# Batch 2's x tiles 0 and 1 turned by DMA instead of TensorE, with its four o tiles planned one to three slots earlier

## The chip, the core and the metric

The kernel runs on one core of one Trainium2 chip. The metric is device time of one execution in microseconds (us): four runs of the kernel before gave 292.17, 292.19, 292.23 and 292.23 us, median 292.21. The granted TensorE clock was 1.0 throughout the profiled execution. Five engines work side by side, each through its own instructions in program order: TensorE (PE, with weight loads shown as PEld), VectorE (DVE), ScalarE (ACT), GpSimd (POOL) and SyncE (SP); here SP does nothing but issue DMAs.

## What is computed

Two stages follow each other. The first is linear attention per batch and head with an RMS norm over each head's 64 features, the second a LayerNorm and a two-layer feed-forward network with ReLU and a residual. The norm's scale commutes with ReLU, so the kernel applies 1/std only at the end (`finish`).

```python
kv  = einsum('bhsd,bhse->bhde', k, v)              # B=8, H=8, S=576, D=64
out = einsum('bhsd,bhde->bhse', q, kv)
x   = out / sqrt(mean(out*out, -1) + 1e-6) * g_norm   # heads side by side: [B, S, 512]
xn  = (x - mean(x)) / sqrt(var(x) + 1e-6) * g_ln
y   = x + relu(xn @ w_ch1) @ w_ch2                 # 512 -> 2048 -> 512
```

## The kernel before

**Tiling.** Each batch has 576 rows: four main tiles of 128 rows and a remainder of 64. The remainders of two neighbouring batches make one more tile (`rem_tile`), and four of these make a ninth block, "rem". A block of four tiles is 512 rows: `x_blk` holds x in float32, `xT_blk` the centred x in bfloat16, turned so that features lie on partitions, and `st_blk` sums for the norm.

**The path of one tile** (class `Tile`). `o` is four PE matmuls into a PSUM bank (L260), from q turned (`qt`) and from the batch's k-v product (`kv_pack`). `sq` squares it on ACT (L266), `red` sums per head on DVE (L287). Then `y` in turn: `rms` on ACT (L297), `inv` (L304) and the multiplication (L292) on DVE; `x` (L311, with L315 for the mean), `xc` (L321), all DVE. `var` is a squared sum on ACT (L329). Last comes `turn`, with two forms:

```python
if on_pe:   # 4 transposes on PE (L337) into the one "misc" bank, copied out by ACT (L339)
else:       nc.sync.dma_start_transpose(dst, self.xc_t)   # one DMA from SP (L341)
```

The turned tile is what the block's first matmul (`mm1`, L402) reads. Its results are cleared through ReLU by ACT (L405) out of three PSUM banks (`ps1`) into `m1`; `mm2` (L418) multiplies those by the second weights into two banks (`ps2`), and `finish` (L423, DVE) makes `o_sb`, which two SP DMAs (L436, L437) store.

**Per batch besides.** `load_batch` on POOL has six DMAs for k, v and q, after a one-element copy (L98, `gate`) that waits until the q of the batch before has been turned. `kv_of` (L235) is 40 PE matmuls and two ACT copies. `turn_q_dma` copies q on DVE (`q_p`, L201) and turns it with one DMA from SP (L203), which gives `qt`.

**The order** is written out by hand. `mm1` and `mm2` are cut into slots: `tick()` stands before each group of 16 matmuls of 128 columns (or 8 of 256, or 4 of 512), and issues whatever the agenda has for that slot number, ahead of the group. `plan_tile(s, make, turn_at, on_pe)` puts `o`, `sq` and `red` into slot s, `y`, `x` and `xc` into s+2, `var` into s+6 and `turn` into slot `turn_at`. Since every engine works in program order, a slot number sets the place on all of them at once.

The slots around the change are: `mm1(1)` 32 to 47, `mm2(1)` 48 to 63 (four slots to an output tile, so `finish` comes ahead of slots 52, 56, 60 and 64), `mm1(2, 0, 2)`, which reads tiles 0 and 1 of batch 2, 64 to 71, and `mm1(2, 2, 2)`, which reads tiles 2 and 3, 72 to 79. In these slots also stand `kv_of(2)` and `turn_q_dma(2)` at 36 and 36.5, `rstd_of(1)` (L410, L411) at 46, `load_batch(3)` at 47, `kv_of(3)` at 55, `turn_q_dma(3)` at 56.7, the remainder tile `rem_tile(1)` at 62 (turned by DMA at 69), batch 3's own o tiles at 65, 70, 75 and 80, and `load_batch(4)` at 68.

Below, t0 to t3 are batch 2's tiles, qt(b) the turned q of batch b, and o_sb(1,n) the n-th output tile of batch 1.

Of the kernel before, what the change touches and what calls it, by code (L numbers as in the profile page):

```python
# [14 lines left out]
def kernel(  # L15
# [183 lines left out]
    def turn_q_dma(b):  # L199
        q_p = kv_in.tile([128, JJ, H, D], bf16, tag="qp", bufs=2)  # L200
        nc.vector.tensor_copy(q_p.rearrange("p j h d -> p h j d"), q_in[b % NB])  # L201
        q_t = qt_pool.tile([128, JJ, HP, 128], bf16, tag="qt", name="qt")
        nc.sync.dma_start_transpose(  # L203
            q_t.rearrange("p j hp t -> p (j hp) t"), q_p.rearrange("p j h d -> p (j h d)"))
        qts[b] = q_t
# [35 lines left out]
    def new_block(n, bufs):  # L241
        x_blk = xpool.tile([128, 4, Dm], f32, tag=f"x{n}", bufs=bufs, name="x_blk")
        st_blk = xpool.tile([128, 3, 4], f32, tag=f"st{n}", bufs=bufs, name="st_blk")
        xT_blk = xpool.tile([128, nK, 512], bf16, tag=f"xT{n}", bufs=bufs, name="xT_blk")
        return x_blk, st_blk, xT_blk
# [98 lines left out]
    def main_tile(b, j, pool=None, tag="ops"):  # L344
        q_t, kvp = qts[b], held[b]
        if b not in blks:
            blks[b] = new_block("main", 3)
        return Tile([(slice(0, 128), lambda hp: q_t[:, j, hp, :], kvp)], blks[b], j, pool, tag)

    def rem_tile(b):  # L350
        mms = []
        for half, bb in enumerate((b - 1, b)):
            qt, kp = qts.pop(bb), held.pop(bb)
            mms.append((slice(half * 64, (half + 1) * 64),
                        lambda hp, qt=qt: qt[:, J, hp, :64], kp))
        if "rem" not in blks:
            blks["rem"] = new_block("rem", 1)
        return Tile(mms, blks["rem"], b // 2)

    def plan_tile(s, make, turn_at, on_pe):  # L360
        box = []

        def first():
            t = make()
            box.append(t)
            t.o()
            t.sq()
            t.red()

        def second():  # L370
            t = box[0]
            t.y()
            t.x()
            t.xc()

        def third():
            box[0].var()

        def fourth():
            box[0].turn(on_pe)  # L380

        at(s, first)
        at(s + 2, second)
        at(s + 6, third)
        at(turn_at, fourth)
# [72 lines left out]
    def at(slot, fn):  # L458
        agenda.setdefault(int(slot), []).append((slot, fn))
# [145 lines left out]

    at(36, lambda: kv_of(2))
    at(36.5, lambda: turn_q_dma(2))
    for j, s, tn in ((0, 46, 53), (1, 51, 58), (2, 55, 63), (3, 59, 68)):
        plan_tile(s, lambda j=j: main_tile(2, j), tn, True)
    plan_tile(62, lambda: rem_tile(1), 69, False)  # L610
    at(78, lambda: rstd_of(2))

    for b in range(3, B):
        s = 32 * b
# [69 lines left out]
```

## Time and profile before

| what | before |
|---|---|
| median of 4 runs | 292.21 us |
| the profiled execution | 292.23 us |
| its span in the profile | 290.4 us |
| PE busy | 280.4 us |
| DVE busy | 150.8 us |
| ACT busy | 155.5 us |
| DMA moved | 35.84 MB |

Times in the profile count from the start of the span; the execution's 292.23 us hold 1.83 us more than the span. A row of the timeline has start, length, engine, line, operation, operands and number of instructions, and in brackets how long the engine sat idle before it and what ended the wait. A PE row's length has the drain of the matmul pipeline in it, so it overlaps the row that follows: what an instruction costs PE is the difference of starts, not the length. The same holds in part for DVE and ACT.

### The profile page before, as it was taken

The page shows a single profiled execution, that of the slowest core. Times are in us where ns is not written, and L with a number is a line of the kernel's source. Part 1 is how long each engine was busy: PE and PEld are TensorE (multiplying, and loading weights), DVE is VectorE, ACT ScalarE, POOL GpSimd, SP SyncE. Part 2 cuts the span into 40 slices and gives each one's busy share as a digit, 9 for nine tenths or more (in the row PEclk, how much of TensorE's full clock was granted, in tenths as well). Part 3 has the DMA queues.
Part 4 walks back from the last instruction along what each step waited for, and adds up shares of the span by engine and source line. Part 5 has one row for each costly group of instructions (what it writes and reads, how often), then busy time and mean ns, then how long its engine had stood idle before and what let it go on. Part 6 is the DMA issues. An engine that isn't in the chain of part 4 may idle for free.

```text
span 290.4 us, 5777 instructions
## 1 busy us (share of the span) xinstructions
PE 280.4 (97%) x2294; PEld 159.4 (55%) x2320; DVE 150.8 (52%) x335; ACT 155.5 (54%) x341; POOL 41.0 (14%) x68
## 2 busy tenths in 40 slices
PE   7789999999999999999999999999999999999995
PEld 3579755995578754444444544444444444444444
DVE  5775028836996893666366935752578300220022
ACT  3467755885569931892189408920894066016500
POOL 8522520032050003200410023000000000000000
PEclk9999999999999999999999999999999999999999
DMA  7999999469789618994997279949202510131033
GB/s 216 203 206 201 201 202 219 105 105 194 141 146 204 100 42 150 211 171 89 150 201 108 49 145 200 165 77 168 54 18 54 110 36 0 38 81 27 2 72 72
DMA packets 63291, 35.84 MB, mean 123 GB/s; under 512 B 30749, under 2 KB 58269, under 8 KB 63265
## 3 DMA queue, kind: packets, MB, share of 16 engines
q0 software_dynamic: 28016, 17.76, 43.8%
q1 hardware_dynamic: 34736, 16.99, 29.4%
q10 hardware_dynamic: 512, 0.72, 0.7%
q8 instruction: 18, 0.29, 0.4%
q14 instruction: 9, 0.07, 0.1%
HBM read 36.71 MB, written 9.44 MB: 159 GB/s over the span
## 4 chain that ended last, share of the span: by engine, by line
PE 84%; DVE 6%; DMA 3%; ACT 2%; issue 2%; POOL 0%; SPq 0%; DVEq 0%; POOLq 0%
PE p L402 40%; PE p L418 38%; DMA v_in<-in_v_dram 2%; PE o_ps L260 2%; PE kv_ps L235 2%; DVE o_sb L423 1%; DVE ss L287 1%; DVE x_blk L311 1%; DVE y L292 1%; DMA out_dram<-o_sb 1%; ACT m L405 1%; PE tp L183 1%; DVE xc L321 1%; PE p L196 1%; ACT sq L266 0%
## 5 line engine op out<-in xcount | busy, mean ns | idle before, releaser
L402 PE MATMUL p<-xT_blk,w_sb 128*128 128x128 bf16 (+2 forms) x1017 | 131.7, 285 | 0.9 <-ACT m L405 0.3
L418 PE MATMUL p<-w_sb,m 128*128 128x512 bf16 (+2 forms) x590 | 126.9, 368 | 1.6 <-issue 0.8
L405 ACT ACTIVATE m<-p 128x512 bf16<-128x512 f32 x144 | 85.3, 597 | 41.8 <-PE p L402 39.7
L402 PEld LDWEIGHTS <-w_sb 128*128 128x128 bf16 x1024 | 78.5, 98 | 44.6 <-issue 1.1
L418 PEld LDWEIGHTS <-m 128*128 128x128 bf16 x608 | 56.8, 98 | 61.2
L423 DVE SCALAR_TENSOR_TENSOR o_sb<-p,rstd,x_blk 128x512 f32<-128x512 f32 (+2 forms) x38 | 27.4, 720 | 54.0 <-PE p L418 51.2
L266 ACT ACTIVATE sq<-o_ps 128x512 f32<-128x512 f32 x34 | 20.2, 595 | 41.2 <-PE o_ps L260 41.2
L329 ACT ACTIVATE dev<-x_blk,st_blk 128x512 f32<-128x512 f32 x36 | 25.7, 715 | 4.5 <-DVE st_blk L315 4.4
L287 DVE TENSOR_REDUCE ss<-sq 128x8 f32<-128x512 f32 x34 | 23.1, 678 | 8.4 <-ACT sq L266 8.4
L321 DVE SCALAR_TENSOR_TENSOR xc<-x_blk,st_blk,g_ln_sb 128x512 bf16<-128x512 f32 x34 | 25.6, 752 | 1.2
L292 DVE TENSOR_TENSOR y<-o_ps,inv 128x512 f32<-128x512 f32 x34 | 23.5, 692 | 2.8
L311 DVE SCALAR_TENSOR_TENSOR x_blk<-y,g_norm_sb 128x512 f32<-128x512 f32 x34 | 23.5, 692 | 1.2
L411 DVE RECIPROCAL rstd<-rstd 128x4 f32<-128x4 f32 x9 | 1.6, 174 | 39.3 <-ACT rstd L410 39.3
L304 DVE RECIPROCAL inv<-rms 128x8 f32<-128x8 f32 x36 | 7.2, 200 | 23.1 <-ACT rms L297 23.1
L98 POOL COPY gate<-qt 1x1 bf16<-1x1 bf16 x5 | 0.9, 178 | 114.8 <-DMA qt<-q_p 114.8
L297 ACT ACTIVATE rms<-ss,eps_sb 128x8 f32<-128x8 f32 x36 | 10.7, 297 | 9.8 <-DVE ss L287 9.1
L260 PEld LDWEIGHTS <-qt 128*128 128x128 bf16 (+1 forms) x152 | 10.0, 100 | 7.3 <-issue 1.7
L260 PE MATMUL o_ps<-kv_pack,qt 128*128 128x128 bf16 (+1 forms) x152 | 13.3, 220 | 0.2 <-DVE qt L191 0.2
L196 PE MATMUL p<-fill_sb 128*128 128x512 bf16 x27 | 8.0, 454 | 1.4 <-DVE eps_sb L137 1.2
L339 ACT COPY xT_blk<-tp 128x512 bf16<-128x512 bf16 x10 | 5.8, 579 | 2.3 <-PE tp L337 2.3
L329 ACT ACTIVATION_READ_ACCUMULATOR dev<-x_blk,st_blk 128x1 f32 x36 | 6.9, 191 | 0.0
L238 ACT CAST kv_pack<-kv_ps 64x256 bf16<-64x256 f32 x7 | 2.6, 366 | 7.2 <-PE kv_ps L235 7.1
(79 smaller groups left out, 118.5 us busy)
## 6 DMA issues: line engine op xcount, KB each, us to landing
out_dram<-o_sb SPq DMA_DIRECT2D x70, 128.0 KB, 2.5
w_sb<-in_moe_w_ch_dram POOLq DMA_DIRECT2D x8, 512.0 KB, 14.0
k_in<-in_k_dram POOLq DMA_DIRECT2D x7, 320.0 KB, 5.5
v_in<-in_v_dram POOLq DMA_DIRECT2D x7, 320.0 KB, 8.6
q_in<-in_q_dram POOLq DMA_DIRECT2D x7, 320.0 KB, 12.7
q_in<-in_q_dram POOLq DMA_DIRECT2D x8, 256.0 KB, 12.5
k_in<-in_k_dram POOLq DMA_DIRECT2D x7, 256.0 KB, 6.5
v_in<-in_v_dram POOLq DMA_DIRECT2D x7, 256.0 KB, 10.1
```

The lines of the kernel that those rows point to most:

```text
L196: nc.tensor.matmul(p1, lhsT=fill_sb[:, :128], rhs=fill_sb, start=True, stop=True)
L260: nc.tensor.matmul(flat[rows, hp * 128:(hp + 1) * 128], lhsT=lhsT_of(hp), rhs=kvp[:, hp, :], start=True, stop=True)
L266: nc.scalar.activation(self.sq_t, self.o_ps, func=AF.Square)
L287: nc.vector.tensor_reduce(self.ss, self.sq_t, axis=AX.X, op=ALU.add)
L292: nc.vector.tensor_mul(self.y_t, self.o_ps, self.inv().to_broadcast([128, H, D]))
L311: nc.vector.scalar_tensor_tensor(x_blk[:, ts].rearrange("p (h d) -> p h d", h=H), in0=self.y_t, scalar=1.0, in1=g_norm_sb.to_broadcast([12 ...
L321: nc.vector.scalar_tensor_tensor(self.xc_t, in0=x_blk[:, self.ts], scalar=st[:, 1, self.ts:self.ts + 1], in1=g_ln_sb, op0=ALU.add, op1=ALU ...
L329: nc.scalar.activation(dev, x_blk[:, ts], func=AF.Square, bias=st[:, 1, ts:ts + 1], accum_out=st[:, 2, ts:ts + 1])
L402: nc.tensor.matmul(p1[:, i, :], lhsT=w1_sb[:, kk, de * 128:(de + 1) * 128], rhs=blk[2][:, kk, sl], start=(kk == 0), stop=(kk == nK - 1))
L405: nc.scalar.activation(m1[:, de0:de0 + per, sl], p1, func=AF.Relu)
L418: nc.tensor.matmul(p2[:, c0:c1], lhsT=m1s[b][:, de, ts * 128:(ts + 1) * 128], rhs=w2_sb[:, de, c0:c1], start=(de == 0), stop=(de == nDe - 1))
L423: nc.vector.scalar_tensor_tensor(o_sb[:, c0:c1], in0=p2[:, c0:c1], scalar=rstds[b][:, ts:ts + 1], in1=blks[b][0][:, ts, c0:c1], op0=ALU.mu ...
```

## The change

Batch 2's four `plan_tile` calls get other slots, and `on_pe` becomes true for t2 and t3 alone.

```diff
-    for j, s, tn in ((0, 46, 53), (1, 51, 58), (2, 55, 63), (3, 59, 68)):
-        plan_tile(s, lambda j=j: main_tile(2, j), tn, True)
+    for j, s, tn in ((0, 44, 50), (1, 48, 54), (2, 53, 61), (3, 58, 67)):
+        plan_tile(s, lambda j=j: main_tile(2, j), tn, j > 1)
```

| tile | `o` slot | `y`, `x`, `xc` | `var` | `turn` | turned by |
|---|---|---|---|---|---|
| t0 | 46 → 44 | 48 → 46 | 52 → 50 | 53 → 50 | PE → SP's DMA |
| t1 | 51 → 48 | 53 → 50 | 57 → 54 | 58 → 54 | PE → SP's DMA |
| t2 | 55 → 53 | 57 → 55 | 61 → 59 | 63 → 61 | PE |
| t3 | 59 → 58 | 61 → 60 | 65 → 64 | 68 → 67 | PE |

On PE the eight transposes and their eight weight loads go, on ACT two copies, and SP gets two DMAs: t0's stands ahead of the stores of o_sb(1,0), t1's between those and the stores of o_sb(1,1). On DVE the order changes too. Before, between `xc` of t0 and the copy `q_p` of batch 3, DVE had: red t1, o_sb(1,0), t1's four operations, red t2, o_sb(1,1), `q_p`. After: red t1, t1's operations, o_sb(1,0), red t2, t2's operations, o_sb(1,1), `q_p`. So t2's inv, y, x and xc now stand ahead of o_sb(1,1) and `q_p`, and not behind them. In the slots of `mm1(1)` t0's `sq` stands on ACT after the second ReLU that follows the last turn of batch 1, two ReLUs earlier than before.

## The prediction

> **What bounds the kernel now.** I read the page's engine row and its chain of waits first, then the timeline of each engine between 54 and 96 us, where batch 2's tiles are made.
>
> ```profile
> PE 280.4 (97%) x2294; PEld 159.4 (55%) x2320; DVE 150.8 (52%) x335; ACT 155.5 (54%) x341; POOL 41.0 (14%) x68
> PE 84%; DVE 6%; DMA 3%; ACT 2%; issue 2%; POOL 0%; SPq 0%; DVEq 0%; POOLq 0%
> ```
>
> PE is busy for 97% of the span, and the chain is PE for 84%. So the time is PE's work plus the gaps in it, and an edit counts only by what it takes off PE or by a gap that it opens or closes. The chain's 6% on DVE lie almost wholly between 67 and 88 us. PE's timeline there:
>
> ```profile
> 81.80 0.38 PE L418 MATMUL p<-w_sb,m 128*128 128x512 bf16 x1
> 82.01 0.39 PE L337 MATMUL tp<-identity,xc 128*128 128x128 bf16 x4
> ...
> 83.10 1.04 PE L402 MATMUL p<-xT_blk,w_sb 128*128 128x256 bf16 x8
> 83.97 0.39 PE L260 MATMUL o_ps<-kv_pack,qt 128*128 128x128 bf16 x4
> 84.19 2.78 PE L402 MATMUL p<-xT_blk,w_sb 128*128 128x256 bf16 x24
> 86.81 0.39 PE L337 MATMUL tp<-identity,xc 128*128 128x128 bf16 x4
> 87.04 1.91 PE L402 MATMUL p<-xT_blk,w_sb 128*128 128x256 bf16 x16
> 88.78 0.39 PE L260 MATMUL o_ps<-kv_pack,qt 128*128 128x128 bf16 x4
> 89.01 1.04 PE L402 MATMUL p<-xT_blk,w_sb 128*128 128x256 bf16 x8
> 90.34 0.92 PE L402 MATMUL p<-xT_blk,w_sb 128*128 128x256 bf16 x7 [0.29 <-ACT m L405]
> ```
>
> Starts tell the price of work on PE. A turn costs 87.04 − 86.81 = 0.23 us, a slot of eight matmuls 83.97 − 83.10 = 0.87. The slot at 89.01 should end at 89.88, and the next starts at 90.34: a gap of 0.46 (the bracket says 0.29, since the drain is counted as busy). ACT's timeline gives its cause:
>
> ```profile
> 87.82 0.30 ACT L297 ACTIVATE rms<-ss,eps_sb 128x8 f32<-128x8 f32 x1 [0.86 <-DVE ss L287]
> 88.03 0.58 ACT L405 ACTIVATE m<-p 128x512 bf16<-128x512 f32 x1
> 88.51 0.58 ACT L339 COPY xT_blk<-tp 128x512 bf16<-128x512 bf16 x1
> ```
>
> `rms` of batch 3's tile 0 waits for a DVE that runs late (its `red` starts at 87.11), and the ReLUs that empty `ps1` queue behind it. DVE is late because t0 to t3, the remainder tile and four stores follow each other without a pause from 73 us, though it did little before (a wait of 5.07 us ends at 65.64).
>
> **The change, part by part.** The sum is made against the profiled execution: 292.23 us, span 290.4 and 1.83 around it; the median is 292.21.
>
> *Two turns leave PE.* Two times 0.23, say 0.45 us. The slots that they leave are full of matmuls, so all of it counts unless a gap takes it. The two ACT copies (0.46 each, 88.97 − 88.51 by starts) were hidden behind PE and count nothing; were ACT the bound there they would be worth 0.9.
>
> (The Trainium skill, "TensorE: Matmul & The Clock Gate", section "Part 4: PE-mode transpose", gives about 275 ns for one 128×128 transpose in a kernel. Eight would be an estimated 2.2 us, and the sum 289.8. The trace's 0.23 us for four pipelined ones decides.)
>
> *t0's `o` two slots earlier* needs qt(2). POOL's `gate` waits for the same landing:
>
> ```profile
> 62.30 0.18 POOL L98 COPY gate<-qt 1x1 bf16<-1x1 bf16 x1 [23.80 <-DMA qt<-q_p]
> ```
>
> A slot of `mm1(1)` costs 0.89 (64 matmuls from 61.05 to 64.62 are four), slot 46 begins at 64.62, so slot 44 begins at 62.84: 0.54 after the landing. Nothing ahead of it changes, so I cost it at nothing; with the longest landing of a qt in the trace (6.9 us in place of 5.0) it would cost 1.4.
>
> *DVE, walked in its new order.* Costs by starts of neighbouring rows: red 0.60, inv 0.31 after a wait (0.23 without), y 0.73, x 0.73, mean 0.19, xc 0.67, o_sb 0.65, q_p 0.74. From `red` to `y` with ACT free it is 0.69 + 0.04 + 0.30 + 0.03 + 0.31 = 1.37. Slot 44's `o` ends at 63.07; `sq` goes behind the ReLU of slot 43, at 63.52, red t0 at 64.14. `rms` is queued behind two ReLUs and `rstd`: 65.74. So y t0 66.37, red t1 68.69, y t1 70.06, o_sb(1,0) 72.38, red t2 73.03, y t2 74.40, o_sb(1,1) 76.72, `q_p` 77.37. Then red t3 78.11, o_sb(1,2) 78.8 (it waits for PE), y t3 79.68, red of the remainder 82.00, o_sb(1,3) 82.87, y 83.75, red of batch 3's tile 0 86.07, where it was 87.11.
>
> So DVE is 1.0 us earlier at the end of the stretch but later in its middle: o_sb(1,1) at 76.72, where it was 75.57. PE needs that bank only in slot 60, at 78.5.
>
> *The 0.46 gap.* `red` ends at 86.76, and the ReLU of slot 67 is ready when PE has done it, at about 87.0. `rms` holds it no longer. Slot 71, at about 89.6, needs the ReLU of slot 68, done by about 89.0. I take the whole 0.46; the other end is nothing. It comes back if DVE is over 0.6 us later than in my walk.
>
> *What is late next: qt(3).* SP issues the stores of o_sb(1,1) and then batch 3's q turn:
>
> ```profile
> 76.34 0.47 SPq L436 DMA_DIRECT2D out_dram<-o_sb  x1
> 76.86 0.59 SPq L437 DMA_DIRECT2D out_dram<-o_sb  x1
> 77.54 3.12 SPq L203 DMA_TRANSPOSE qt<-q_p  x1
> ```
>
> POOL's next `gate` again shows the landing:
>
> ```profile
> 82.62 0.18 POOL L98 COPY gate<-qt 1x1 bf16<-1x1 bf16 x1 [15.75 <-DMA qt<-q_p]
> ```
>
> The turn is issued 1.20 us after the first store's issue and seen 5.08 later. With o_sb(1,1) done at 76.72 + 0.74 = 77.46, the issue is at 78.7 and qt(3) there at 83.77. PE wants it for slot 65, before at 83.97, now 0.45 earlier, at 83.52. That is a new wait of 0.25 us. Below, it can be nothing; above, with the 6.9 us landing, it is 2.1. I take 0.25, because the row at 77.54 is this very transfer with the same neighbours on SP. `load_batch(4)` starts 1.1 us later by it, but `kv_of(4)` needs its data only at 101.88, and the slowest v landed at 85.61 + 9.2 = 94.8.
>
> *The two turns as DMAs.* xc t0 ends at about 68.8, and its turn goes out at once; behind it in SP's order wait the stores of o_sb(1,0), not ready before 73.1. Those come ahead of t1's turn, which so leaves at 73.1 + 1.2 = 74.3, and not at 72.4 when xc t1 is done. Of the 24 such turns in the trace one lands in 2.4 to 9.0 us; the two issued during the load of batch 4 took 7.3. That gives 76.1 for t0 and 81.6 for t1. `mm1(2)` reads them at 82.65, so I cost both at nothing; at 9.0 us t1 would stop PE for 0.65.
>
> *The load of batch 3.* Its last v transfer is issued at 64.80 and lands 7.4 us later, at 72.2; `kv_of(3)` needs it at about 73.1. In the load of batch 4, which had two turns and two stores amid it, the same transfer took 9.2. Cost: nothing to 0.9; I take nothing, because t0's turn alone can fall ahead of 72.2. q lands at 66.14 + 9.1 = 75.2, 2.1 ahead of `q_p`.
>
> (The Trainium skill, "DMA: Bandwidth & Descriptors", section "Queues, rings and completion order", has each DMA engine take turns between the queues that hold work. That speaks against a turn amid a load: by it v would wait for up to t0's 128 KB, about 0.7 us at the 195 GB/s of that stretch, an estimate, and land at 72.9. The sum by it is the same as mine.)
>
> **Sum:** 292.23 − 0.45 − 0.46 + 0.25 = 291.57 us.
>
> **The rivals.** *The middle eats it.* DVE or the landing is some half a us later than in my walk: qt(3) takes the whole 0.45, and the ACT gap stays or PE merely shifts it. For it: four hand-overs between ACT and DVE lie in the walk, each with a few hundredths unknown, and slot 65 has no slack at all. Against: every price is a row of this trace. Time: 292.23 − 0.45 + 0.45 − 0.2 = 292.0, between 291.7 and 292.6.
>
> *qt(3) comes far too late, and the kernel is slower.* One mechanism: batch 3's q turn at SP goes out while other traffic (t1's turn, stores, the delayed end of the load) still fills the engines, and lands as the worst one did. With 6.9 us it is there at 85.6, PE waits 2.1 in slot 65, and the time is 292.23 − 0.91 + 2.1 = 293.4. It decides from a landing 0.9 us after 83.52, at 84.4. For it: t1's turn and two pairs of stores now go out within the 5 us ahead of it. Against: the load ended at 75.2, and before, qt(3) came 5.1 us after issue just behind stores.
>
> That the turns stay on PE is excluded: `on_pe` is false for both.
>
> **How the numbers follow.** My forecast, 291.57, has 0.53, with 291.3 to 291.7 as its own range (291.3 is both gains whole and no wait). The middle has 0.32, the slow case 0.15. A change of 0.2%, 0.58 us, is about what a measurement of this kernel tells from none: faster means below 291.63. Nearly all of the forecast's chance lies there; a little of it, and most of the middle's, counts as the same. So faster 0.51, same 0.34, slower 0.15. The range of 8 in 10 runs from 291.25 through the middle case to 292.4.
>
> **What would show it.** On PE eight transposes fewer, and no wait for ACT at about 89.9; a wait of 0.1 to 0.4 us ahead of batch 3's first `o` at about 83.6, put down to a DMA or as unexplained; `red` of batch 3's tile 0 near 86.1; the copy `q_p` near 77.4 and L203 near 78.7; both new L341 landed before 82.6. I am wrong if PE stops at slot 55 for v or at slot 64 for a turn, if the wait for qt(3) exceeds half a us, or if new gaps appear behind 91 us.

## The result, and the profile after

The changed kernel takes 291.75 us (median of 39 runs, 291.58 at the lowest), the kernel before 292.25 in the same comparison (60 runs). The ratio is 0.998, with a 95% interval of 0.9974 to 0.9987: a gain of 0.50 us. The profiled execution took 291.62 us with a span of 289.5. The page's engine row and chain:

```profile
span 289.5 us, 5765 instructions
PE 280.7 (97%) x2286; PEld 158.8 (55%) x2312; DVE 151.1 (52%) x335; ACT 154.9 (54%) x339; POOL 41.2 (14%) x68
PE 93%; DMA 2%; issue 1%; ACT 1%; DVE 1%; POOL 0%; POOLq 0%
```

The chain was 84% PE and 6% DVE; now it is 93% PE and 1% DVE. The stretch in which DVE set the pace is gone. PE's timeline at the places that the prediction spoke of:

```profile
82.58 1.04 PE L402 MATMUL p<-xT_blk,w_sb 128*128 128x256 bf16 x8
83.61 0.40 PE L260 MATMUL o_ps<-kv_pack,qt 128*128 128x128 bf16 x4
83.84 1.91 PE L402 MATMUL p<-xT_blk,w_sb 128*128 128x256 bf16 x16
...
88.43 0.39 PE L260 MATMUL o_ps<-kv_pack,qt 128*128 128x128 bf16 x4
88.66 4.53 PE L402 MATMUL p<-xT_blk,w_sb 128*128 128x256 bf16 x40
```

Slot 64 takes 83.61 − 82.58 = 1.03 us where eight such matmuls take 0.87: this is the new wait for qt(3), 0.16 us. The matmuls' rows have no bracket for it, but the weight load ahead of them names what it waited for:

```profile
83.60 0.23 PEld L260 LDWEIGHTS <-qt 128*128 128x128 bf16 x4 [0.27 <-DMA qt<-q_p]
```

From 88.66 on forty matmuls run without a break, through slot 71, where the 0.46 us gap was. ACT shows why:

```profile
86.28 0.58 ACT L339 COPY xT_blk<-tp 128x512 bf16<-128x512 bf16 x1
86.75 0.31 ACT L297 ACTIVATE rms<-ss,eps_sb 128x8 f32<-128x8 f32 x1
86.95 0.60 ACT L405 ACTIVATE m<-p 128x512 bf16<-128x512 f32 x1
```

`rms` no longer waits for DVE (before, 0.86 us idle stood ahead of it). SP and POOL:

```profile
68.72 1.20 SPq L341 DMA_TRANSPOSE xT_blk<-xc  x1
73.05 0.48 SPq L436 DMA_DIRECT2D out_dram<-o_sb  x1
73.58 0.59 SPq L437 DMA_DIRECT2D out_dram<-o_sb  x1
74.22 2.19 SPq L341 DMA_TRANSPOSE xT_blk<-xc  x1
77.38 0.47 SPq L436 DMA_DIRECT2D out_dram<-o_sb  x1
77.89 0.60 SPq L437 DMA_DIRECT2D out_dram<-o_sb  x1
78.58 3.18 SPq L203 DMA_TRANSPOSE qt<-q_p  x1
```

```profile
83.68 0.18 POOL L98 COPY gate<-qt 1x1 bf16<-1x1 bf16 x1 [16.89 <-DMA qt<-q_p]
```

The turns landed 8.6 and 3.7 us after issue, at 77.3 and 77.9, both well ahead of 82.58. qt(3) is there at 83.68.

Times between executions shift at the start of the kernel, so the experiments are read by one **stage**: from the start of batch 1's last turn on PE to the start of batch 3's third `o`. Before it is 93.86 − 60.83 = 33.03 us, after 93.02 − 60.75 = 32.27: 0.76 saved. There is one traced execution of each program, so one stage of each; where two programs should agree, their stages do so within 0.02 us. The traced executions of experiments 1, 4 and 7 lasted 1.1 to 1.3 us longer than the medians of their runs, most of it ahead of the stage (it begins at 62.21, 61.57 and 62.11 there, elsewhere at 60.8 or 60.9); in all three the median span moves as the stage does, within 0.1 us. The whole span shows 0.9. The execution shows 0.5 to 0.6. So something outside the span takes a part back; the last four experiments are about that.

### The profile page after: what moved, and what is told of

It is laid out like the page before. It is cut to its first block, busy times and chain, and to the rows that moved or that the text cites. A ratio compares the mean times of both kernels' runs of the same rounds, so it can differ in the third digit from the quotient of the medians.

```text
span 289.5 us, 5765 instructions
## 1 busy us (share of the span) xinstructions
PE 280.7 (97%) x2286; PEld 158.8 (55%) x2312; DVE 151.1 (52%) x335; ACT 154.9 (54%) x339; POOL 41.2 (14%) x68
## 4 chain that ended last, share of the span: by engine, by line
PE 93%; DMA 2%; issue 1%; ACT 1%; DVE 1%; POOL 0%; POOLq 0%
PE p L418 43%; PE p L402 42%; PE o_ps L260 3%; DMA v_in<-in_v_dram 2%; PE kv_ps L235 2%; PE tp L183 1%; PE tp L337 1%; PE p L196 1%; ACT sq L266 0%; PE tp L170 0%; DVE xc L532 0%; PE o_half L500 0%; POOL v_in L126 0%; ACT m L405 0%; DVE x_blk L278 0%
## 5 line engine op out<-in xcount | busy, mean ns | idle before, releaser
L196 PE MATMUL p<-fill_sb 128*128 128x512 bf16 x27 | 8.8, 487 | 1.4 <-DVE eps_sb L137 1.2
L235 PEld LDWEIGHTS <-k_in 128*64 128x64 bf16 x280 | 5.0, 112 | 2.6 <-issue 2.5
```

Source lines behind the costliest of these rows:

```text
L196: nc.tensor.matmul(p1, lhsT=fill_sb[:, :128], rhs=fill_sb, start=True, stop=True)
```

## The experiments

The first eight are read by the stage and by their medians. "Around" is the median of an execution's time less its span; before it is 1.78 us, after 2.15. Of most edits only the lines that go in are shown.

| run | stage, us | span | around | median, us | ratio to before, interval |
|---|---|---|---|---|---|
| before | 33.03 | 290.5 | 1.78 | 292.25 | |
| after | 32.27 | 289.6 | 2.15 | 291.75 | 0.998, 0.9974 to 0.9987 |
| slots only | 32.55 | 290.0 | 1.98 | 291.99 | 0.9994, 0.9981 to 1.0006 |
| DMA only | 32.51 | 289.8 | 2.01 | 291.81 | 0.9983, 0.9974 to 0.9991 |
| q turn first | 32.10 | 289.45 | 2.15 | 291.62 | 0.9985, 0.9968 to 1.0002 |
| all four by DMA | 32.75 | 290.15 | 1.88 | 292.01 | 0.9993, 0.9983 to 1.0003 |
| t1 alone by DMA | 33.02 | 290.4 | 1.78 | 292.16 | 0.9998, 0.9989 to 1.0007 |
| t0 alone by DMA | 32.50 | 289.9 | 1.78 | 291.63 | 0.9984, 0.997 to 0.9998 |
| copy behind rms | 32.73 | 290.2 | 1.78 | 291.95 | 0.9986, 0.9974 to 0.9997 |
| q turn first, t2 by DMA | 31.88 | 289.2 | 1.79 | 291.01 | 0.9959, 0.9944 to 0.9974 |

(Spans of runs are medians over their executions.)

### 1. The slots alone

```diff
+    for j, s, tn in ((0, 44, 53), (1, 48, 58), (2, 53, 61), (3, 58, 67)):
+        plan_tile(s, lambda j=j: main_tile(2, j), tn, True)
```

> The four o tiles in the new slots, all four turns on PE (t0 at 53, t1 at 58, t2 at 61, t3 at 67). My theory: the 0.46 us gap for ACT at slot 71 goes, since DVE's order is that of the changed kernel; the two turns cost PE their 0.45 again, and with PE that much later batch 3's first o no longer waits for qt(3). So 0.46 under before and a little over the changed kernel: 291.8 us (291.7 to 291.9). Rival, the turns taken off PE are what pays and the slots only make room for them: 292.2 us, as before.

The stage is 32.55, 0.48 under before, and PE has no wait for ACT in it: the gap went, the turns stayed. That is the theory's 0.46. The median fell by only 0.25, because the time around the span grew by 0.2, which I had not allowed for. The interval of this run holds 1: by the medians alone this run would be inconclusive.

### 2. The DMAs alone

```diff
+    for j, s, tn in ((0, 46, 50), (1, 51, 54), (2, 55, 63), (3, 59, 68)):
+        plan_tile(s, lambda j=j: main_tile(2, j), tn, j > 1)
```

> The o tiles in the slots of before, t0 and t1 turned by DMA (at slots 50 and 54), t2 and t3 as before. My theory: DVE still ends the stretch as late as before, so ACT and then PE wait at slot 71 for the same moment; the 0.45 us that PE saves goes into that gap, which grows from 0.46 to about 0.9, and the time stays at 292.2 us (292.1 to 292.3). Rival, PE's work is the bound and the turns count by themselves: 291.8 us.

The theory missed: 291.81 and a stage of 32.51, so 0.52 saved in the old slots too. But the rival's reason is not shown by it either, since most of the gap at slot 71 is still there (PE starts that slot at 89.86 after one that began at 88.60, a gap of 0.39). PE still waited there, so what moved slot 71 has to be what it waited for, and behind that stands DVE. ACT before, between the squares of t1 and t2:

```profile
70.76 0.19 ACT L329 ACTIVATION_READ_ACCUMULATOR dev<-x_blk,st_blk 128x1 f32 x1
71.60 0.59 ACT L339 COPY xT_blk<-tp 128x512 bf16<-128x512 bf16 x1 [0.65 <-PE tp L337]
72.08 0.30 ACT L297 ACTIVATE rms<-ss,eps_sb 128x8 f32<-128x8 f32 x1
```

and in this run:

```profile
70.79 0.19 ACT L329 ACTIVATION_READ_ACCUMULATOR dev<-x_blk,st_blk 128x1 f32 x1
71.04 0.30 ACT L297 ACTIVATE rms<-ss,eps_sb 128x8 f32<-128x8 f32 x1
```

Before, t0's turn on PE has its copy on ACT ahead of `rms` of t1. ACT idles 0.65 us for PE and copies for 0.48 while t1's sums have lain ready since 70.97, and DVE's next tile waits for that `rms`:

```profile
72.42 0.20 DVE L304 RECIPROCAL inv<-rms 128x8 f32<-128x8 f32 x1 [0.80 <-ACT rms L297]
```

Without the turn `rms` starts 1.04 us earlier and `inv` 0.84 (71.58, before 72.42). So my view became: in the old slots DVE sets slot 71, and the copy held DVE. Experiments 5 to 7 test it: the first two against the view that PE's saved work counts by itself, the third against the view that the order on ACT does not matter.

### 3. The q turn ahead of the stores

```diff
-        at(s + d + 1.7, lambda b=b: turn_q_dma(b))
+        at(s + d + (0.7 if b == 3 else 1.7), lambda b=b: turn_q_dma(b))
```

> The changed kernel with turn_q_dma(3) one slot earlier (55.7), so that q_p stands on DVE, and the q turn on SP, ahead of the store of o_sb(1,1). My theory: q_p at 76.6, the q turn issued at 77.4 and qt(3) there at 82.5, 1 us before PE wants it at 83.45; the wait of 0.16 us at slot 65 goes and nothing comes for it: 291.6 us (291.5 to 291.65). Rival, the wait is no cost of its own (PE would wait for something else there): 291.75 us. If q of batch 3 has not landed by 76.6, q_p stops DVE and the time is above 291.75.

The stage is 32.10, 0.17 under the changed kernel, and `o` follows slot 64 after 0.88 us. The wait for qt(3) was a cost of its own. The median, 291.62, lies where the theory had it, though its interval alone does not part it from either kernel.

### 4. All four tiles by DMA

```diff
+    for j, s, tn in ((0, 44, 50), (1, 48, 54), (2, 53, 58), (3, 58, 62)):
+        plan_tile(s, lambda j=j: main_tile(2, j), tn, False)
```

> The changed kernel with t2 and t3 turned by DMA too (at slots 58 and 62). On SP both stand behind the q turn and its 3.2 us of issue, so t2's goes out at about 81.8 and t3's at about 84.2, just as the load of batch 4 starts. My theory: PE saves another 0.45 us, if t3's turn lands by slot 72, at about 90: 291.3 us; each us by which it lands later (8 to 9 us in a load, so 92 to 93) is added: up to 293.5. Rival, a turn amid a load is as quick as outside one (2.4 us): 291.3 us for sure.

```profile
84.60 0.40 PE L260 MATMUL o_ps<-kv_pack,qt 128*128 128x128 bf16 x4 [0.40 <-DMA qt<-q_p]
...
91.70 2.78 PE L402 MATMUL p<-xT_blk,w_sb 128*128 128x256 bf16 x24 [0.37 <-DMA xT_blk<-xc]
```

Here PE's timeline names both waits: for qt(3), and at slot 72 for t3's turn, which SP issued at 85.28. Late, as the theory feared, but by half a us and not by 2 or 3. The stage is 32.75, worse than the changed kernel's by 0.48: the further turns took 0.45 us of work off PE and were paid back in waits, 0.40 more for qt(3) and 0.54 at slot 72 (91.70 − 89.42 − 2 × 0.87).

### 5 to 7. Who moves slot 71

t1 alone by DMA, in the old slots:

```diff
+    for j, s, tn in ((0, 46, 53), (1, 51, 54), (2, 55, 63), (3, 59, 68)):
+        plan_tile(s, lambda j=j: main_tile(2, j), tn, j != 1)
```

> The kernel before with t1 alone turned by DMA (at slot 54), old slots. I judge by the stage from the start of batch 1's last turn to the start of batch 3's third o (33.03 us before, 32.51 with both turns as DMAs in the old slots, 32.27 in the changed kernel), since the time around the span differs from program to program (1.78 to 2.15 us). Theory now: slot 71 is set by DVE, and DVE is ahead in the run with both turns because t0's PE turn held ACT: its copy waits for PE ahead of rms of t1. t1's turn holds nobody. So the 0.22 us that PE saves goes into the gap: stage 33.0 us, span 290.4. Rival, PE's savings count by themselves: stage 32.8 us, span 290.2.

t0 alone:

```diff
+    for j, s, tn in ((0, 46, 50), (1, 51, 58), (2, 55, 63), (3, 59, 68)):
+        plan_tile(s, lambda j=j: main_tile(2, j), tn, j != 0)
```

> The kernel before with t0 alone turned by DMA (at slot 50), old slots. Theory now: without t0's copy ACT does rms of t1 as soon as red is done, DVE runs about 0.5 us earlier, and slot 71 follows it though PE saves only 0.22: stage 32.5 us, span 289.9, as with both turns. Rival, PE's savings count by themselves: stage 32.8 us, span 290.2.

No DMA, t0's copy behind `rms` of t1:

```diff
+    for j, s, tn in ((0, 46, 53.5), (1, 51, 58), (2, 55, 63), (3, 59, 68)):
+        plan_tile(s, lambda j=j: main_tile(2, j), tn, True)
```

> The kernel before with t0's turn left on PE and in slot 53, but issued behind the second part of t1 in that slot, so that on ACT its copy stands behind rms of t1; nothing else differs, no DMA is added and no work leaves PE. Theory now: inv of t1 goes from 72.4 to about 71.6; o_sb(1,1) then waits for PE at about 75.3 (75.57 before), so DVE gains 0.26 and the gap at slot 71 shrinks to 0.2: stage 32.8 us, span 290.15. Rival, the order of that copy does not matter: stage 33.03 us, span 290.4.

With t1 alone PE does 0.22 us less and gains nothing: 33.02. PE's timeline has the saving as a longer wait:

```profile
88.83 1.04 PE L402 MATMUL p<-xT_blk,w_sb 128*128 128x256 bf16 x8
90.37 0.82 PE L402 MATMUL p<-xT_blk,w_sb 128*128 128x256 bf16 x6 [0.51 <-ACT m L405]
```

90.37 − 88.83 − 0.87 = 0.67, before 0.46. With t0 alone the same 0.22 us off PE gives 0.53: 32.50, as much as both turns. And with no work taken off PE, the order of two ACT instructions gives 0.30: 32.73, a ratio of 0.9986 whose interval, 0.9974 to 0.9997, excludes 1. All three came out as the view had it. What ties the stage to DVE is the place of `red` of batch 3's tile 0, counted from the stage's start: in every program with the old slots it moves as the stage does.

| old slots | stage, us | `red` of batch 3's tile 0, from the stage's start | o_sb(1,1), from the stage's start |
|---|---|---|---|
| before | 33.03 | 26.28 | 14.74 |
| t1 alone | 33.02 | 26.28 | 14.74 |
| copy behind `rms` | 32.73 | 25.99 | 14.44 |
| t0 alone | 32.50 | 25.76 | 14.22 |
| both (experiment 2) | 32.51 | 25.76 | 14.22 |

The last column says why t0's turn counts fully and t1's not at all. Once the copy no longer holds DVE, o_sb(1,1) waits for PE (the row is that of t0 alone):

```profile
74.99 0.75 DVE L423 SCALAR_TENSOR_TENSOR o_sb<-p,rstd,x_blk 128x512 f32<-128x512 f32 x1 [0.29 <-PE p L418]
```

t0's turn on PE lies ahead of that point, so its 0.22 us are added to the 0.30; t1's lies behind it. ACT with the copy behind `rms`:

```profile
72.28 0.30 ACT L297 ACTIVATE rms<-ss,eps_sb 128x8 f32<-128x8 f32 x1
72.88 0.58 ACT L339 COPY xT_blk<-tp 128x512 bf16<-128x512 bf16 x1 [0.30 <-PE tp L337]
```

### 8. The best version

The q turn at 55.7 as in 3, and t2 by DMA, t3 on PE:

```diff
+    for j, s, tn in ((0, 44, 50), (1, 48, 54), (2, 53, 58), (3, 58, 67)):
+        plan_tile(s, lambda j=j: main_tile(2, j), tn, j == 3)
```

> The changed kernel with turn_q_dma(3) at 55.7 (which took the stage to 32.10 us) and t2 turned by DMA too (slot 58), t3 on PE. Theory: SP issues t2's turn at about 81.8, behind the q turn and two stores; even at the 7.3 us of a turn amid a load it lands by 89.1, ahead of slot 72 at about 89.3, so PE saves 0.22: stage 31.88 us, span 289.2. Rival, it lands as the slowest (9 us) and PE waits at slot 72: stage 33 us.

```profile
77.50 3.08 SPq L203 DMA_TRANSPOSE qt<-q_p  x1
80.68 0.54 SPq L436 DMA_DIRECT2D out_dram<-o_sb  x1
81.27 0.59 SPq L437 DMA_DIRECT2D out_dram<-o_sb  x1
81.91 1.29 SPq L341 DMA_TRANSPOSE xT_blk<-xc  x1
```

t2's turn went out at 81.91 and landed in 2.5 us, ahead of the next load. The stage is 31.88, exactly the sum, and the median 291.01: 1.2 us under before in its own comparison, 0.7 under the changed kernel. About half of the latter lies around the span (1.79 us, not 2.15).

### 9 to 12. The time around the span

The records of semaphores reach beyond the span: behind the last instruction about 250 of them are updated one after another, and the last eight updates all go to one semaphore. I read the first as their being set back and the second as a barrier; the records give neither values nor engines. Of the barrier's last five updates the second comes 0.10 us after the first before, but 0.46 after the change (from 1.71 to 2.17 us behind the span's end); the others keep their distances. Among the first eight experiments only "q turn first" shows such a step too (0.45), and these two programs have the same number of recorded instructions on SP, DVE and PE's sequencer, which no other shares. So each of four engines got one idle instruction in slot 150 of the changed kernel, each in a run of its own; all four have the spare 128x1 tile, and all but PE's write into it:

```diff
+    spare = consts.tile([128, 1], f32)
+    at(150, lambda: nc.vector.memset(spare, 0.0))       # DVE
+    at(150, lambda: nc.scalar.copy(spare, eps_sb))      # ACT
+    at(150, lambda: nc.sync.dma_start(spare, eps_sb))   # SP
...
+        nc.tensor.matmul(p1[:, :64], lhsT=fill_sb[:, :128], rhs=fill_sb[:, :64], start=True, stop=True)   # PE
```

> The changed kernel with one idle memset of 128x1 on DVE added in slot 150, where DVE has nothing urgent. The question is the time around the span: 2.15 us in the changed kernel and in the run with the q turn first, 1.78 before and in four others, with the last step of the barrier behind the span at 0.46 us in those two and 0.10 in all others. Theory: it depends on where one engine's code ends, since these two programs have the same number of instructions on every engine and no other has theirs on SP, PE and DVE. If DVE's code is the one, the time around the span falls to about 1.8 us and the time to 291.35; if not it stays at 2.15 and 291.7. Rival, it is a cost of the change itself (more DMAs to close): 2.15 in all four of these runs.

> The changed kernel with one idle copy of 128x1 on ACT added in slot 150. Two programs with the changed kernel's number of ACT instructions had 1.78 us around the span, so if the place of code decides, it is not ACT's: 2.15 us stays, 291.7 us. If it falls to about 1.8, the count of instructions is not what decides.

> The changed kernel with one matmul of 64 columns, whose result nobody reads, added on PE in slot 150 (0.03 to 0.2 us of work). If PE's code is the one that ends late, the time around the span falls from 2.15 to about 1.8 us, otherwise it stays.

> The changed kernel with one DMA of 512 bytes from SBUF to SBUF, which nobody reads, added on SP in slot 150. If SP's code is the one that ends late, the time around the span falls from 2.15 to about 1.8 us, otherwise it stays. If the number of DMAs were the cost, it would rise.

| one instruction more on | around, us | barrier step | median, us |
|---|---|---|---|
| DVE | 1.78 | 0.10 | 291.17 |
| ACT | 2.17 | 0.45 | 291.52 |
| PE | 2.15 | 0.45 | 291.49 |
| SP | 2.15 | 0.45 | 291.60 |

One memset on DVE takes 0.37 us off the time around the span; on the other engines nothing changes. So the rival, a cost of two more DMAs, falls. All 14 programs agree on what the step goes with: the five whose trace records 440 instructions on DVE's queue (after, "q turn first", and those with one more on ACT, PE or SP) have 0.45 or 0.46, and the nine with 436, 437, 438, 441 or 442 have 0.10. So it hangs on DVE's program, and not simply on its length, since longer and shorter ones are both quick. That DVE is the engine that arrives late at the barrier fits this but is not shown, and that its code is fetched late at that point is only a guess; no record shows the fetch. Nor is it explained that "slots only" and "DMA only" have 0.2 us more around their spans than before, and "all four by DMA" 0.1: their barrier step is 0.10.

All four are also faster within the span: the stage is 32.10 in each, 0.17 under the changed kernel. The q turns are shorter:

```profile
L203 SPq DMA_TRANSPOSE qt<-q_p x6: 2501/2611/2688, 57.2 to 193.2; - x6
DMA to landing us min/median/max: 4.1/4.2/6.4
```

This is the line's summary in the run with one more on ACT (durations in ns: least, median, most). In the changed kernel the six have a median of 3154 ns, and land in 5.0 us. The q turns are shorter from the first on, at 57.2 us, and slot 150, where the added instructions stand, comes long after (162.8 us on ACT). What the four have in common ahead of that is the spare tile of four bytes a partition, which can shift whatever is allocated behind it. The wait for qt(3) goes in all four (in the run with one more on ACT qt(3) is there at 83.02, in the changed kernel at 83.68). That the place in memory does it is thus argued and not shown, and whether the place of `q_p` or of `qt` matters was not tried apart.

## Why the prediction held, and where it did not

*Two turns leave PE, 0.45.* As large as predicted: the stage with the slots alone, 32.55, less 0.45 and plus the wait of 0.16 gives 32.26, and 32.27 was measured. (The 275 ns for one transpose from the Trainium skill, "TensorE: Matmul & The Clock Gate", section "Part 4: PE-mode transpose", would have made an estimated 2.2 us of the eight; the runs show a fifth of it.)

*The 0.46 gap goes.* Right in size and in place: 0.48 in the run with the slots alone. DVE's walk held to 0.15 us: y t0 was put at 66.37 and came at 66.28, o_sb(1,1) at 76.72 and came at 76.60, `red` of batch 3's tile 0 at 86.07 and came at 85.99.

*The wait for qt(3), 0.25.* Right in cause and sign, 0.16 in the profiled execution. The q turn went out at 78.58 (predicted 78.7) and was there at 83.68 (83.77). The 0.09 too much is nearly all in how the landing was read: the prediction took it from POOL's `gate`, which starts 0.08 us later than PE's weight load for the same landing (83.68, 83.60).

*The turns as DMAs and the load, nothing.* Right: PE had no wait at slots 55 and 64. t0's turn took 8.6 us amid the load, not the 7.3 that I took, and t1's 3.7. The last v transfer landed 7.4 us after issue as before, so t0's turn did not delay it; the last q transfer took 9.9 in place of 9.1. (The Trainium skill, "DMA: Bandwidth & Descriptors", section "Queues, rings and completion order", has the engines take turns between queues that hold work; by the rule alone v was estimated to land about 0.7 us later, and this trace shows nothing of that for v. Whether the last q transfer's 0.8 us come from it was not tested.)

*The two ACT copies, "hidden behind PE and count nothing".* This step was wrong for the old slots. It asked only whether ACT was the bound, and not what stood behind the copy in ACT's order. There it held `rms` of t1 and with it DVE, worth 0.30 by itself (experiment 7). It did no harm to the forecast, because with the new slots DVE is early enough either way (experiment 1 has the copies and no gap).

*1.83 us around the span.* The step that made the difference of 0.18 between the forecast and the result. The sum took the time around the span to be fixed; by the medians it rose by 0.37, from 1.78 to 2.15, in the last barrier, and experiment 9 takes it back with one DVE instruction. Against that stand a wait 0.09 shorter than predicted and a span that gained about 0.15 more than the stage, for which no run shows a cause; that these two offset most of it is luck. The median, 291.75, so lies 0.05 above the forecast's own range (291.3 to 291.7) and above the 291.63 that the prediction called faster. It falls where the middle case had its range, but not for that case's reason.

The middle case, in which the wait for qt(3) takes everything, did not come about, but its margin was 0.3 us. Experiment 4 shows how near it is: the same wait grows to 0.56 (84.60 − 83.17 − 0.87), 0.22 of that because PE comes earlier without t2's turn, and a second one follows. The slow case, a q turn landing in 6.9 us, did not occur at that place in any trace.

## What to carry to other kernels

Before counting work taken off a busy engine, ask what stands behind each of its helpers' instructions: here a copy that waited for PE stood ahead of a short instruction on which another engine's next tile hung, and swapping the two gave 0.30 us with no work taken away, while taking another 0.22 us off the busy engine gave nothing. Saved work on the bound engine counts only up to the next wait that something else sets (with t1 alone, up to the one at slot 71). And when effects are some tenths of a us, compare a stage within the trace besides the total, since the total holds an ending that can change with one instruction.

## What the runs showed of the hardware that was not expected

The time around the span belongs to the program and hardly varies between its executions: 1.73 to 1.84 us in 35 executions before, 2.09 to 2.22 in 40 after, with spans given to 0.1 us. One idle DVE instruction of 128x1 and its target tile made the changed kernel about half a us faster (291.17 us where its comparison had 292.18 for before, against 291.75 and 292.25): 0.37 of it by the last barrier, the rest within the span, where the spare tile's four bytes a partition came, in all four programs that have it, with q turns of 2.6 us of issue in place of 3.15.
